# A fused attention and two-network kernel: a 32x32 inverse kept in PSUM, background work handed out by time, and filler matmuls two by two at two points

## The chip, the cores and the metric

One NeuronCore of one Trainium2 chip. The metric is the device time of one execution in microseconds (us); several executions are taken and their median is compared. The profile is one further execution, taken by the hardware profiler.

## What is computed

A linear-recurrence attention over 4 batches of 8 heads, 768 tokens, head width 40 (so 320 columns per token), and then two feed-forward networks on all 3,072 tokens:

```
for t in range(S):
    y[:, :, t] = einsum('bhd,bhde->bhe', rt, state)
    Sa = einsum('bhde,bhe->bhd', state, at)
    state = state * wt[:, :, None, :] - einsum('bhd,bhe->bhde', Sa, bt)
    state = state + einsum('bhd,bhe->bhde', vt, kt)
x = (sigmoid(y @ w_gate) * (y @ w_val)) @ w_out          # 320 -> 1536 -> 320
h = x @ w_in; e = exp(h - max(h)); u = h * e / sum(e)    # 320 -> 1024
out = layernorm(u) * g_ln @ w_out2                       # 1024 -> 320
```

## The kernel before, in words

**Slots.** The recurrence is done in 24 chunks of 32 tokens (`CH`), each for two halves of the heads, so in 48 half-chunks. `Attention.slot(s)` is written out for s from -6 to 48: slot s does the dependent part of half-chunk s and, ten slots ahead (`LOOK`), the preparation of a later one. A slot is a list `work` of ten points: 0 `m_r` and `m_st`; 1 and 2 the two halves of `m_ruv` of the half-chunk before, whose result VectorE masks into RL (L370); 3 `m_u` (ScalarE copies its PSUM result into Z at L312); 4 and 5 `products` of half-chunk s+9; 6 `m_y`, which reads RL; 7 `m_state`, which reads Z; 8 `m_ut`, `natural` and loads; 9 nothing. All engines work through their own instructions in the order in which the program issues them, and SyncE's queue issues the DMAs in that order.

**The inverse.** Each pair of chunks (n = 0 to 11, two chunks each) needs a 32x32 triangular inverse per head and chunk. `products` gives the matrices, ScalarE copies them to `abn` (L218), a DMA stores them to `ab`, and `t_load` loads them back as M (L526) in the layout that the inverse wants. `eye` loads a unit matrix from DRAM into the SBUF tile TT (two buffers). `t_iter(n, j)`, j = 0 to 30, does on VectorE one multiplication (L260: PSUM tile pT <- TT times M, both in SBUF) and one addition (L264: TT <- TT plus pT) on (j//2+1)*(31-j) columns. For n = 0 and 2 each is cut into two instructions from j = 6 on; for n = 1 VectorE takes the first two rows and GpSimd the rest (with an SBUF tile `tmp`). `t_store` writes TT to DRAM (L270), and `t_fetch` (L284) loads it as TB for `m_u`. `SOLVE` says which j are done in which of the four slots k = 0 to 3 that precede the use of inverse n; k = (s+5) mod 4.

**The background list.** `back` is a slot's list of VectorE work that no matmul of this slot waits for: the inverse's instructions and, in slots with k = 2 and 3, ahead of them, the four steps of `decay` (a clamp L144, two scans L154 and L161, two small ones). At each of the ten points the same number of items is handed out (`share`, the rest divided by the points left). In the k = 0 slot twelve empty items stand first, so that M has time to arrive. The list goes to `Between.fill`, which mixes it with the conversion of weights (`Convert.value`: four VectorE instructions L600 to L605 and two, L606 and L607, on the engine `cv.eng`, which is VectorE up to slot 2 and GpSimd after).

**The first network's units.** From slot 6 on, `fill` also puts in units of the first network for tokens that are finished: `units` yields in turn a gate (8 matmuls, L820), a value (8 matmuls, then a sigmoid on ScalarE L840 and a product on VectorE L841) and a third that splits the product (ScalarE L536, GpSimd L537) and does the 6 output matmuls (L853 to L855) of the tile before. One unit stands at each of the points `UNITS`; where none is ready, two dummy matmuls. After slot 48 the rest of the first network (`Late.tail`, `Late.first`) and the second (`Late.second`) follow.

Of the kernel before, what the change touches and what calls it, by code (L numbers as in the profile page):

```python
# [68 lines left out]
class Attention:  # L69
    def __init__(self, tc, ctx, d, xT, abd, ttd, bad, ident, zero, memory):  # L70
# [172 lines left out]

    def t_load(self, n):
        nc = self.nc
        M = self.sb.tile([128, CH, CH], F32, tag="M", name=f"M{n}", bufs=2)
        twice(nc, M.rearrange("p j t -> p (j t)"), self.abd[n])
        self.T[n] = (M, self.T.get(n) or self.eye(n))

    def t_iter(self, n, j):  # L250
# [5 lines left out]
        cut = min(m, T1) if n == 1 else m // 2 if m >= 4 and n in (0, 2) else 0
        parts = [(nc.vector, slice(0, cut), self.pT), (nc.gpsimd if n == 1 else nc.vector, slice(cut, m), self.tmp if n == 1 else self.pT)][cut == 0:1 + (cut < m)]

        def mult(eng, r, tmp):
            eng.tensor_tensor(out=tmp[:, 0:m * k].rearrange("p (c t) -> p c t", t=k)[:, r], in0=TT[:, r, j:j + 1].broadcast_to([128, r.stop - r.start, k]),  # L260
                              in1=M[:, j:j + 1, j + 1:CH].broadcast_to([128, r.stop - r.start, k]), op=ALU.mult)
# [1246 lines left out]
```

## Time and profile before

| | |
|---|---|
| Runs | 1168.12, 1170.61, 1173.04 us: median 1170.61 us |
| The profiled execution | 1175.68 us, of it 1173.9 us from first to last instruction |
| Busy share of the span | TensorE 88%, VectorE 72%, ScalarE 50%, GpSimd 41% |
| Slots 7 to 34 | from 197.3 to 538.9 us |
| Slots 39 to 47 | from 581.6 to some 664 us |
| Last part, without attention | from 684.0 us on |

Times in the profile count from the span's start. In the lines of groups the columns are: line, engine, operation, output <- inputs by the program's names, shapes, count | busy time in us, mean of one in ns | idle time of the engine before them and what ended it.

### The profile page before, as it was taken

The page shows a single profiled execution, that of the slowest core. Times are in us where ns is not written, and L with a number is a line of the kernel's source. Part 1 is how long each engine was busy: PE and PEld are TensorE (multiplying, and loading weights), DVE is VectorE, ACT ScalarE, POOL GpSimd, SP SyncE. Part 2 cuts the span into 40 slices and gives each one's busy share as a digit, 9 for nine tenths or more (in the row PEclk, how much of TensorE's full clock was granted, in tenths as well). Part 3 has the DMA queues.
Part 4 walks back from the last instruction along what each step waited for, and adds up shares of the span by engine and source line. Part 5 has one row for each costly group of instructions (what it writes and reads, how often), then busy time and mean ns, then how long its engine had stood idle before and what let it go on. Part 6 is the DMA issues. An engine that isn't in the chain of part 4 may idle for free.

```text
span 1173.9 us, 31891 instructions
## 1 busy us (share of the span) xinstructions
PE 1038.1 (88%) x12710; PEld 885.7 (75%) x12710; DVE 845.6 (72%) x2099; ACT 582.7 (50%) x1487; POOL 486.8 (41%) x529
## 2 busy tenths in 40 slices
PE   5527868898988989899999989799999998999997
PEld 2414546787877979788889878688888876888897
DVE  8969999999989898999894236234443359676673
ACT  4215534566656656656666435233443343544552
POOL 7628652644556455565321112144344301222232
PEclk8557987999999899989999989989999999999999
DMA  6455644667768665785564144312211000000001
GB/s 181 130 129 138 159 91 110 163 157 185 188 164 197 162 173 149 174 221 139 136 158 124 58 116 138 102 29 88 82 47 45 1 1 6 18 23 18 18 23 38
DMA packets 181037, 125.53 MB, mean 107 GB/s; under 512 B 106192, under 2 KB 159440, under 8 KB 180880
## 3 DMA queue, kind: packets, MB, share of 16 engines
q1 hardware_dynamic: 180880, 123.40, 40.1%
q8 instruction: 103, 1.69, 0.6%
q14 instruction: 54, 0.44, 0.1%
HBM read 101.83 MB, written 21.53 MB: 105 GB/s over the span
## 4 chain that ended last, share of the span: by engine, by line
PE 57%; DVE 24%; DMA 7%; ACT 4%; SPq 4%; issue 3%; POOL 1%; ACTq 0%; DVEq 0%; POOLq 0%
PE hid L820 20%; DVE pT L260 6%; PE one L820 5%; DVE TT L264 3%; PE pY L383 3%; PE two L853 2%; PE pruv L366 2%; PE three L1191 2%; PE three L1194 2%; PE three L1192 2%; PE two L855 2%; PE two L854 2%; PE two L1178 2%; PE pABK L206 2%; DVE G L161 2%
## 5 line engine op out<-in xcount | busy, mean ns | idle before, releaser
L260 DVE TENSOR_TENSOR pT<-TT,M 128x30 f32<-128x30 f32 (+38 forms) x422 | 161.2, 382 | 15.6 <-DMA TT<-in_ceye_dram 7.0
L820 PE MATMUL hid<-l_x,l_w 128*128 128x512 f32 x672 | 161.4, 392 | 0.0
L820 PEld LDWEIGHTS hid<-l_x,l_w 128*128 128x128 f32 x672 | 125.4, 189 | 24.4 <-issue 0.2
L820 PE MATMUL one<-b_tokens,b_w 128*128 128x256 f32 x816 | 125.2, 296 | 2.1 <-DVE b_plain L841 2.1
L223 POOL TENSOR_TENSOR AT<-abn,mA 64x256 f32<-64x256 f32 x96 | 79.4, 827 | 102.5 <-ACT abn L218 95.1
L820 PEld LDWEIGHTS one<-b_tokens,b_w 128*128 128x128 f32 x816 | 104.4, 191 | 7.7 <-DVE b_plain L841 2.3
L537 POOL TENSOR_TENSOR l_x<-l_plain,l_x 128x512 fp32r<-128x512 f32 x43 | 55.7, 1295 | 118.9 <-ACT l_x L536 99.9
L264 DVE TENSOR_TENSOR TT<-TT,pT 128x30 f32<-128x30 f32 (+38 forms) x422 | 94.6, 233 | 12.0
L841 DVE TENSOR_TENSOR l_plain<-hid,l_plain 128x512 f32<-128x512 f32 x43 | 29.7, 691 | 95.6 <-ACT l_plain L840 95.5
L383 PE MATMUL pY<-RL,YR 128*64 128x32 f32 (+1 forms) x1536 | 62.7, 226 | 39.8 <-DVE RL L370 38.3
L537 POOL TENSOR_TENSOR b_tokens<-b_plain,b_tokens 128x256 fp32r<-128x256 f32 x58 | 45.3, 780 | 123.2 <-ACT b_tokens L536 119.2
L820 PE MATMUL hid<-b_w,l_x 128*128 128x512 f32 x384 | 94.0, 397 | 2.6 <-DVE l_e L1150 2.6
L383 PEld LDWEIGHTS pY<-RL,YR 128*64 128x64 f32 (+1 forms) x1536 | 55.6, 137 | 51.7 <-issue 24.6
L820 PEld LDWEIGHTS hid<-b_w,l_x 128*128 128x128 f32 x384 | 70.9, 188 | 19.0 <-DVE l_e L1150 3.4
L206 PE MATMUL pABK<-AT,BK 128*64 128x64 f32 x768 | 62.8, 240 | 22.5 <-POOL BK L196 21.6
L195 POOL TENSOR_TENSOR AT<-AT,G 40x256 f32<-40x256 f32 x90 | 75.3, 837 | 15.6 <-DMA AT<-in_LA_dram 12.4
L206 PEld LDWEIGHTS pABK<-AT,BK 128*64 128x64 f32 x768 | 54.8, 151 | 33.9 <-POOL BK L196 24.2
L536 ACT ACTIVATE b_tokens<-b_plain 128x256 fp32r<-128x256 f32 (+1 forms) x70 | 33.7, 489 | 87.3 <-DVE b_plain L841 64.0
L312 ACT ACTIVATE Z<-pu 32x160 f32<-32x160 f32 x192 | 56.7, 295 | 34.4 <-PE pu L309 31.8
L840 ACT ACTIVATE l_plain<-hid 128x512 f32<-128x512 f32 x43 | 25.7, 597 | 96.5 <-PE hid L820 96.4
L935 PE MATMUL one<-zero 128*128 128x512 bf16 x196 | 66.7, 450 | 1.3 <-DVE lim L96 1.3
L1185 POOL TENSOR_TENSOR l_w<-l_e,l_w 128x1024 fp32r<-128x1024 f32 x12 | 28.8, 2403 | 89.1 <-ACT l_e L1146 51.1
(254 smaller groups left out, 2614.0 us busy)
## 6 DMA issues: line engine op xcount, KB each, us to landing
AT<-in_LA_dram SPq DMA_DIRECT2D x48, 256.0 KB
RL<-in_RS_dram SPq DMA_DIRECT2D x24, 512.0 KB
LB<-in_LB_dram SPq DMA_DIRECT2D x46, 208.0 KB
Z<-in_VN_dram SPq DMA_DIRECT2D x48, 160.0 KB
M<-ab SPq DMA_DIRECT2D x24, 256.0 KB
UV<-in_VT_dram SPq DMA_DIRECT2D x24, 208.0 KB
G<-in_LW_dram SPq DMA_DIRECT2D x22, 214.5 KB
xT<-yt SPq DMA_DIRECT2D x24, 160.0 KB
```

Of the source, the lines that this page charges most:

```text
L195: eng.tensor_tensor(out=at[SROW[g], g], in0=at[SROW[g], g], in1=G[SROW[g]], op=ALU.mult)
L206: yield lambda m=m: nc.tensor.matmul(ps[0:64, m * 64:m * 64 + 64], lhsT=bkt[:, m].rearrange("p s t -> p (s t)"), rhs=at[:, :, m, :], start ...
L223: nc.gpsimd.tensor_tensor(out=at[UROW[g], g].rearrange("p (a b) t -> p a b t", a=2), in0=abn[UROW[g], :, hs], in1=self.mA[UROW[g]].unsquee ...
L260: eng.tensor_tensor(out=tmp[:, 0:m * k].rearrange("p (c t) -> p c t", t=k)[:, r], in0=TT[:, r, j:j + 1].broadcast_to([128, r.stop - r.star ...
L264: eng.tensor_tensor(out=TT[:, r, j + 1:CH], in0=TT[:, r, j + 1:CH], in1=tmp[:, 0:m * k].rearrange("p (c t) -> p c t", t=k)[:, r], op=ALU.add)
L312: nc.scalar.activation(z[32 * q:32 * q + 32, hs, g, p * 4:p * 4 + 4, :], ps[32 * q:32 * q + 32, 0:160].rearrange("p (h d) -> p h d", d=40) ...
L383: yield lambda m=m, g=g, at=at: nc.tensor.matmul(ps[rows[g], m * CH:m * CH + CH], lhsT=flat[:, at:at + rows[g].stop - rows[g].start], rhs= ...
L536: nc.scalar.activation(h, src, AF.Copy)
L537: eng_l.tensor_tensor(out=l, in0=src, in1=h.bitcast(F32), op=ALU.subtract)
L820: nc.tensor.matmul(out, lhsT=a, rhs=b, start=n == 0, stop=n == 7)
L841: self.nc.vector.tensor_tensor(out=self.sg, in0=self.pv, in1=self.sg, op=ALU.mult)
L935: self.nc.tensor.matmul(self.gv, lhsT=z[:, 0:128], rhs=z, start=True, stop=True)
```

## The change

- `pT`, the PSUM tile of one bank, holds the inverse itself; the products go to one of two SBUF tiles `tmp`. So each multiplication reads PSUM and SBUF and writes SBUF, and each addition reads PSUM and SBUF and writes PSUM, in place.
- The unit matrix is loaded once into an SBUF tile and copied into pT by ScalarE (`eye`); `t_store` copies pT to SBUF by ScalarE, lets ScalarE write the next unit matrix, and stores as before. For n >= 1 it becomes an item of `back` in the k = 3 slot, behind the inverse's last step; for n = 1 that is slot 2 in place of slot 3.
- Inverse 1 is done by VectorE alone, in whole instructions; the conversions' last two instructions go to GpSimd in all slots.
- `back` carries an estimated time for each item, and each point gets its share of the remaining time (items are taken until the share is used up). The twelve empty items become one of 2.0 us. The steps of `decay` stand behind the inverse's, no longer ahead of them. `SOLVE` for n >= 3 gives 12, 12, 4 and 3 steps to k = 0 to 3 in place of 6, 9, 8 and 8. Counted through for n >= 3: in a k = 0 slot the empty item fills point 0 and the inverse begins at point 1; in k = 2 and 3 slots the inverse's instructions fill points 0 to 2 or 0 and 1, `t_store` stands at point 2 of k = 3, and `decay` at points 2 to 5.
- `m_state` at the end of a pair of chunks adds in place in PSUM, and the product with PE reads that PSUM tile.
- `UNITS` becomes (2, 2, 9, 9): two units at point 2 and two at point 9.

```diff
-SOLVE = (0, 0, 13, 26, 31), (0, 0, 11, 21, 31), (0, 6, 15, 23, 31)
-T1 = 2
-STORE = 5
+SOLVE = (0, 0, 13, 26, 31), (0, 0, 11, 21, 31), (0, 12, 24, 28, 31)
+WAIT = 2.0
-UNITS = (2, 5, 7, 9)
-LAST = {-2: (2, 7, 9), -1: (2, 7, 9), 0: (2,)}
+UNITS = (2, 2, 9, 9)
+LAST = {-2: (2, 9, 9), -1: (2, 9, 9), 0: (2,)}
...
-    def eye(self, n):
-        TT = self.T[n] = self.sb.tile([128, CH // 2, CH], F32, tag="TT", name=f"TT{n}", bufs=2)
-        self.nc.sync.dma_start(out=TT.rearrange("p j t -> p (j t)"), in_=self.d["ceye"])
-        return TT
+    def eye(self):
+        self.nc.scalar.activation(self.pT, self.unit, AF.Copy)
...
+        M, TT = self.M[n], self.pT.rearrange("p (j t) -> p j t", t=CH)
         k, m = CH - 1 - j, j // 2 + 1
+        tmp = self.tmp[j % 2][:, 0:m * k].rearrange("p (c t) -> p c t", t=k)
+        cut = m // 2 if m >= 4 and n in (0, 2) else 0
+        parts = [r for r in (slice(0, cut), slice(cut, m)) if r.stop > r.start]
+        def mult(r):
+            nc.vector.tensor_tensor(out=tmp[:, r], in0=TT[:, r, j:j + 1].broadcast_to([128, r.stop - r.start, k]),
+                                    in1=M[:, j:j + 1, j + 1:CH].broadcast_to([128, r.stop - r.start, k]), op=ALU.mult)
+        def add(r):
+            nc.vector.tensor_tensor(out=TT[:, r, j + 1:CH], in0=TT[:, r, j + 1:CH], in1=tmp[:, r], op=ALU.add)
+        return [(0.155 + (r.stop - r.start) * k * 0.00104, lambda r=r, f=f: f(r)) for f in (mult, add) for r in parts]
...
     def t_store(self, n):
+        self.M.pop(n)
+        TT = self.sb.tile([128, CH // 2, CH], F32, tag="TT", name=f"TT{n}", bufs=1)
+        self.nc.scalar.activation(TT.rearrange("p j t -> p (j t)"), self.pT, AF.Copy)
+        if n + 1 < NSS:
+            self.eye()
...
-            nc.vector.tensor_tensor(out=o, in0=ps[SROW[g], 0:320].rearrange("p (n d) -> p n d", d=40), in1=z[SROW[g], hs, g], op=ALU.add)
+            nc.vector.tensor_tensor(out=sums if end else o, in0=sums, in1=z[SROW[g], hs, g], op=ALU.add)
-                nc.vector.tensor_tensor(out=o, in0=o, in1=pe.unsqueeze(2).broadcast_to([40, 8, 40]), op=ALU.mult)
+                nc.vector.tensor_tensor(out=o, in0=sums, in1=pe.unsqueeze(2).broadcast_to([40, 8, 40]), op=ALU.mult)
...
-                back += [None] * (12 if s >= 0 else 0)
+                back += [(WAIT, None)]
...
+            if k == 2 * SS - 1:
+                back += [(0.0, lambda: self.t_store(n))]
...
-                back = self.decay(m, hs) + back
+                back += zip((0.5, 1.3, 0.4, 1.3), self.decay(m, hs))
...
-            share = -(-len(back) // (len(work) - p))
-            fill(s, back[:share])
-            back = back[share:]
+            share, left = [], sum(x for x, _ in back) / (len(work) - p)
+            while back and (left > 0 or p == len(work) - 1):
+                x, f = back.pop(0)
+                share.append(f)
+                left -= x
+            fill(s, share)
...
-            self.cv.eng = self.nc.vector if s < 3 else self.nc.gpsimd
+            self.cv.eng = self.nc.gpsimd
```

## Rows read from the trace of the kernel before

**Rows 1.** Busy time by stretch (from:to, length; PE, PEld, DVE, ACT, POOL; PEclk, DMA):

```profile
31.50:64.40 32.90, 15.94 (x128) 10.86 (x126) 29.94 (x114) 8.72 (x21) 15.85 (x20) 0.60 0.43 113
81.20:197.30 116.10, 89.00 (x1279) 56.93 (x1278) 108.69 (x290) 56.35 (x165) 69.50 (x103) 0.84 0.55 138
197.30:538.90 341.60, 310.85 (x5905) 275.59 (x5904) 315.57 (x824) 213.30 (x638) 191.96 (x222) 0.93 0.66 168
...
306.90:317.30 10.40, 10.40 (x217) 9.46 (x217) 9.88 (x30) 7.68 (x24) 5.36 (x7) 1.00 0.59 163
329.00:345.10 16.10, 12.10 (x214) 11.00 (x214) 15.45 (x41) 9.66 (x30) 8.62 (x10) 0.89 0.48 136
```

**Rows 2.** Who waited for whom (us in total, times, longest):

```profile
PE pY L383 <- DVE RL L370: 38.3, 18, 4.9
...
ACT b_tokens L536 <- DVE b_plain L841: 64.0, 32, 8.9
```

**Rows 3.** Timeline of TensorE: `m_y` of slot 18, and the start of slot 39:

```profile
338.81 1.63 PE L383 MATMUL pY<-RL,YR 128*64 128x32 f32 x32 [2.72 <-DVE RL L370]
...
581.61 0.49 PE L295 MATMUL pr<-Z,AT 128*32 128x40 f32 x32
```

**Rows 4.** The chain that ended last, in order of time (start, length):

```profile
65.07 2.91 DMA tt<-TT
...
137.34 3.34 DMA tt<-TT
...
583.12 4.26 DMA M<-ab
```

**Rows 5.** Timeline of GpSimd and VectorE, the same shape early and later:

```profile
32.98 1.18 POOL L196 TENSOR_TENSOR BK<-LB,Q 104x512 f32<-104x512 f32 x1
...
33.21 1.03 DVE L260 TENSOR_TENSOR pT<-TT,M 128x58 f32<-128x58 f32 x1
...
82.20 0.23 DVE L260 TENSOR_TENSOR pT<-TT,M 128x58 f32<-128x58 f32 x1
...
82.46 0.22 DVE L264 TENSOR_TENSOR TT<-TT,pT 128x58 f32<-128x58 f32 x1
```

**Rows 6.** The inverse's two groups on VectorE from 31.5 to 64.4 us:

```profile
L260 DVE TENSOR_TENSOR pT<-TT,M 128x60 f32<-128x60 f32 (+33 forms) x56 | 20.5, 365 | 1.9
...
L264 DVE TENSOR_TENSOR TT<-TT,pT 128x60 f32<-128x60 f32 (+33 forms) x56 | 9.4, 205 | 1.1
```

**Rows 7.** Groups of VectorE from 81.2 to 197.3 us:

```profile
L260 DVE TENSOR_TENSOR pT<-TT,M 128x60 f32<-128x60 f32 (+32 forms) x81 | 32.4, 400 | 8.7 <-DMA TT<-in_ceye_dram 7.0
L264 DVE TENSOR_TENSOR TT<-TT,pT 128x60 f32<-128x60 f32 (+31 forms) x79 | 14.1, 198 | 1.3
...
L607 DVE TENSOR_TENSOR b_raw<-b_plain 128x384 f32<-128x384 f32 (+1 forms) x5 | 2.8, 553 | 0.0
```

**Rows 8.** The inverse's additions over one whole inverse, 296.4 to 345.1 us:

```profile
L264 DVE TENSOR_TENSOR TT<-TT,pT 128x126 f32<-128x126 f32 (+22 forms) x32 | 8.0, 250 | 1.1
```

**Rows 9.** Groups of VectorE from 197.3 to 538.9 us:

```profile
L260 DVE TENSOR_TENSOR pT<-TT,M 128x126 f32<-128x126 f32 (+23 forms) x221 | 84.5, 382 | 2.8
L264 DVE TENSOR_TENSOR TT<-TT,pT 128x126 f32<-128x126 f32 (+24 forms) x222 | 54.9, 249 | 7.4
...
L332 DVE TENSOR_TENSOR Z<-Z,PE 40x320 f32<-40x320 f32 x29 | 19.6, 675 | 1.0
```

**Rows 10.** A group of ScalarE, PSUM to SBUF, 512 columns:

```profile
L840 ACT ACTIVATE l_plain<-hid 128x512 f32<-128x512 f32 x43 | 25.7, 597 | 96.5 <-PE hid L820 96.4
```

**Rows 11.** Timeline of slot 16: `m_u`, ScalarE's copies, `m_y`'s successor `m_state`:

```profile
310.00 0.49 PE L309 MATMUL pu<-rn,TB 32*32 32x40 f32 x32
...
310.56 1.25 ACT L312 ACTIVATE Z<-pu 32x160 f32<-32x160 f32 x4 [0.44 <-PE pu L309]
...
313.69 0.81 PE L326 MATMUL pS<-Z,YR 64*40 64x40 f32 x32
```

**Rows 12.** The page's group of gate and value matmuls (8 to a unit):

```profile
L820 PE MATMUL one<-b_tokens,b_w 128*128 128x256 f32 x816 | 125.2, 296 | 2.1 <-DVE b_plain L841 2.1
```

More of the change, by code (lines that the diff above doesn't have):

```diff
@@ L91, in __init__ @@
         self.pT = py.tile([128, 512], F32, name="pT")
-        self.tmp = cp.tile([128, 160], F32, name="tmp")
+        self.unit = cp.tile([128, 512], F32, name="unit")
+        self.tmp = [cp.tile([128, 160], F32, name=f"tmp{i}") for i in range(2)]
         self.QB = [cp.tile([104, 8, WCOLS], F32, name=f"Q{i}") for i in range(3)]
@@ L105, in __init__ @@
         nc.sync.dma_start(out=self.ident, in_=d["cid"])
+        nc.sync.dma_start(out=self.unit, in_=d["ceye"])
         nc.sync.dma_start(out=self.mA, in_=d["cmA"].rearrange("p (n t) -> p n t", t=CH))
@@ L250, in t_iter @@
     def t_iter(self, n, j):
         nc = self.nc
-        M, TT = self.T[n]
+        M, TT = self.M[n], self.pT.rearrange("p (j t) -> p j t", t=CH)
         k, m = CH - 1 - j, j // 2 + 1
[L256 to L261, printed above, removed]
@@ L263, in add @@
-        def add(eng, r, tmp):
-            eng.tensor_tensor(out=TT[:, r, j + 1:CH], in0=TT[:, r, j + 1:CH], in1=tmp[:, 0:m * k].rearrange("p (c t) -> p c t", t=k)[:, r], op=ALU.add)
-        return [lambda x=x, f=f: f(*x) for f in (mult, add) for x in parts]
-    def t_store(self, n):
-        M, TT = self.T.pop(n)
+        tmp = self.tmp[j % 2][:, 0:m * k].rearrange("p (c t) -> p c t", t=k)
+        cut = m // 2 if m >= 4 and n in (0, 2) else 0
+        parts = [r for r in (slice(0, cut), slice(cut, m)) if r.stop > r.start]
@@ L328, in m_state @@
             o = zn[SROW[g], hs, g]
[L329 to L330 removed]
+            end = c % SS == SS - 1
+            sums = ps[SROW[g], 0:320].rearrange("p (n d) -> p n d", d=40)
+            nc.vector.tensor_tensor(out=sums if end else o, in0=sums, in1=z[SROW[g], hs, g], op=ALU.add)
+            if end:
                 pe = self.PE[c // SS + 1, hs][SROW[g]]
[L332 removed]
+                nc.vector.tensor_tensor(out=o, in0=sums, in1=pe.unsqueeze(2).broadcast_to([40, 8, 40]), op=ALU.mult)
     def m_ut(self, i):
@@ L479, in slot @@
                 self.t_load(pj // (2 * SS))
-            if s == 3 and p == STORE:
-                self.t_store(1)
             if p == 4 and s % 2 and 3 < s < NHS - 1:
@@ L488, in slot @@
                     self.w_sums(m, hs)
-            share = -(-len(back) // (len(work) - p))
-            fill(s, back[:share])
-            back = back[share:]
-        if 1 < n < NSS and k == 3:
-            self.t_store(n)
+            share, left = [], sum(x for x, _ in back) / (len(work) - p)
[4 more added lines that the diff above has]
+            fill(s, share)
         if s == -3:
@@ L955, in fill @@
         b, k = divmod(s - FILL, 4)
-        if p in LAST.get(s - NHS, UNITS) and not self.step(b):
-            self.dummy(IDLE)
+        for _ in range(LAST.get(s - NHS, UNITS).count(p)):
+            if not self.step(b):
+                self.dummy(IDLE)
         mix(self.jobs2.next if not self.jobs2.over() or self.jobs2.todo else lambda: next(flat.run, None), LATER[self.jobs2.over()][p], other)
```

13 lines of the change are left out of this document (4 added, 9 removed).

## The prediction

> **What bounds the kernel now.** I read the stretches first, then the waits, then the chain and the timeline inside each stretch. Three stretches hang on VectorE. From 31.5 to 64.4 us it does inverse 0 almost alone, busy 29.9 of 32.9 us. From 81.2 to 197.3 us (slots 0 to 6) it is busy 108.7 of 116.1 us, and in slots 7 to 34 315.6 of 341.6 us [rows 1]. A slot that runs freely takes 10.4 us, all of it TensorE at full clock; slot 18 takes 16.1 us, with VectorE busy for 15.45 and the granted clock at 0.89 [rows 1]. The place where TensorE loses it is point 6: `m_y` waits for RL 18 times, 38.3 us in all [rows 2], 2.72 us of it in slot 18 [rows 3], because the two masks behind `m_ruv` stand in VectorE's queue behind `decay` and the inverse. So 28 slots at 10.4 us, 291 us, is TensorE's floor for the long stretch, and VectorE's load is what keeps the kernel 50 us above it. In the first stretch the chain runs through inverse 0 into its store at 65.07 us [rows 4], and SyncE's queue, with everything behind that store, stands until then. After 538.9 us TensorE rules, and the change leaves that part as it is but for nine slots.
>
> **Why a multiplication is dear.** A multiplication of 58 columns at 33.21 us took 1.03 us and ended when GpSimd's instruction beside it had ended (32.98 + 1.18 = 34.16); the same shape at 82.20 us took 0.23 us, and the addition of that shape, which reads PSUM and SBUF, 0.22 us [rows 5]. The additions' means in the groups below stay at that level in stretches where GpSimd is busy half the time and more. So the cost is two SBUF inputs beside GpSimd, and the change takes exactly that away: no instruction of the inverse has two SBUF inputs any more. I price each new multiplication as an addition of its shape.
>
> **First stretch.** Inverse 0: 56 multiplications of 365 ns become 56 of 205 ns [rows 6], 56 x 0.160 = **-9.0 us**, all on the chain. (The additions' busy time is 9.4 us and not 56 x 0.205 = 11.5, so pairs overlap; if multiplications came to overlap as well, it would be 11.1: one end of the range.) ScalarE's copy out of PSUM before the store costs 0.6 us by a copy of 512 columns [rows 10], **+0.6**. The copy of the unit matrix into PSUM has no row; the nearest is that same 0.6 us. It lies behind the store's copy, off the chain, where ScalarE waits for SyncE's queue anyway. The unit matrix for inverse 1 no longer comes by a DMA: VectorE waited 7.0 us for it [rows 7]. M is issued just ahead of it in the same queue, so most of that wait stays: **-1**, bounds 0 and -7.
>
> **Slots 0 to 6.** Inverses 1 and 2 cost VectorE 32.4 + 14.1 = 46.5 us [rows 7]. After: inverse 1 whole and on VectorE alone is two times a whole inverse's additions, 2 x 8.0 [rows 8]; inverse 2 in halves is, like inverse 0, 2 x 11.5. 39.0 in all, -7.5. L606 and L607 leave VectorE, twice 2.8 us [rows 7], -5.6. The four products with PE lose some 0.2 us each, as below. **-14 us** of 108.7; with VectorE 94% busy I take all of it off the span. GpSimd, busy 69.5 of 116 [rows 1], loses its share of inverse 1 and gets those conversions, so it is no new bound. The store of inverse 1 comes a slot earlier; its 3.34 us on the chain [rows 4] may go (0 to -3.3, I take 0, as VectorE fills the time).
>
> **Slots 7 to 34.** 221 multiplications cost 84.5 us, as many additions 54.9: -29.6. L332 takes 675 ns for 320 columns with two SBUF inputs [rows 9]; with one in PSUM I take 490, from the additions' slope, -5.3. VectorE's busy time becomes 280.7; with the same 26 us idle, 307 us, above TensorE's 291. So it can give 35 us, 50 if VectorE stopped mattering. The order helps: RL no longer has two scans in front of it but a few small instructions, so the waits of rows 2 should nearly go, and `decay`, now behind RL, has a whole slot before GpSimd's products need it. Three things take back. (1) M: the wait of 2.0 us fills one point only, so the inverse begins at point 1, where it began at about 4. For inverse 11 M landed at 583.12 + 4.26 = 587.38, 5.8 us after its slot began [rows 3, 4], and point 1 comes some 1.3 us after that start (`m_r` takes 0.49, as much again for the transposes). RL stands behind that wait. Bounds 0 and 4.5 us for each of 7 inverses; I take 0.7, near the low end, as VectorE runs behind TensorE wherever it is the bound: 5 us. (2) The store's copy stands at point 2 of a k = 3 slot on ScalarE, waits for the last addition, and has `m_u`'s copies to Z behind it; 0 to 1.6 us each, I take 0.2. (3) Pairing: where a value and the splitting unit now stand at one point, ScalarE's split waits for VectorE's product at once; it waits 64 us now [rows 2], hidden. Between the end of `m_u` and `m_state` there were 3.2 us and the copies needed 1.3 [rows 11]; a unit of 8 matmuls, 125.2/102 = 1.2 us [rows 12], leaves this gap, so 2.0 stay: 0.7 to spare, no cost, with point 9's and point 2's covers longer by one unit. Sum **-29 us**.
>
> **Slots 38 to 47.** From slot 39 `products` are gone and `m_u` to `m_state` has `m_y` alone, some 1.0 us (3.2 less the unit and the products), against 1.3: +0.3 in each of nine, **+2.5**; the earlier store of inverse 11 gives **-1**.
>
> **Sum.** -9.0 + 0.6 - 1 - 14 - 29 + 2.5 - 1 = -50.9. The profiled execution took 1175.7 us (span 1173.9), 5.1 above the median; it would take 1124.8, and the median of 1170.6 becomes **1120**.
>
> **Rivals.**
> (a) PSUM costs more. Against: the 0.22 and 0.23 us of rows 5 are the same with and without a PSUM input. If each of the 56 + 87 + 222 multiplications took 65 ns more, 24 us would go back: 1144, chance 0.06. [...]
> (b) Reading and writing one PSUM bank in the same addition runs at half pace; no row shows such an instruction. An inverse's additions stream for 8.0 - 31 x 0.155 = 3.2 us; ten inverses on the chain give back 32: 1152, chance 0.08.
> (c) M is the next bound: 4.5 us for 7 inverses in place of 0.7, 27 back: 1147. For: the landing of inverse 11. Against: between `m_ruv` and `m_y` TensorE has some 3.8 us of work (two units 2.4, `m_u` 0.5, products 0.9). Chance 0.18.
> (d) **Slower**: ScalarE's queue at point 3. The gap there shrinks to 2.0 us, and the copies to Z may start late behind the split of a unit put at point 2. Each of the 33 slots 6 to 38 stalls by what the lateness has over 0.7 us; at 2.2 us the whole gain is spent, at 3 us it is 33 x 2.3 = 76: 1196. Against: in slot 16 the copies began 0.07 us after `m_u` ended [rows 11]. Chance 0.06.
> (e) The list does not hand out what it says, since VectorE's lengths depend on GpSimd; then the waits of the long stretch stay, and of its 29 us only L332's 5 are left: 24 back, 1144, chance 0.05.
> (f) VectorE stops mattering in slots 7 to 34: 21 us more, 1099, chance 0.07.
>
> **How the numbers follow.** The forecast has 0.50. Its own range, 1106 to 1134, comes from the overlap of pairs (-2), the unit matrix (-6), the store of inverse 1 (-3.3), and M and ScalarE (up to +14). The range of 8 in 10 takes in (a), (c), (e) and (f) and stops short of (b) and (d): 1098 to 1150. A measurement can tell some 0.5%, 6 us. Faster 0.90; slower, (d), 0.06; within 0.5%, where (b) and (c) come together, 0.04.
>
> **What would show it.** L260's mean at about the additions' 205 to 250 ns in all three stretches, beside GpSimd too (else a; L264 grown means b); inverse 0's store some 8 us earlier; the wait of `m_y` for RL nearly gone and slots of k = 2 and 3 near 10.4 to 11.5 us at full clock; no large wait of L260 for M (else c), of L326 for Z (else d). The forecast is wrong if VectorE's busy time falls by 35 us in slots 7 to 34 and the stretch does not.

## The result: 0.9% slower, with the profile after

The median of the changed kernel is 1181.1 us (1178.0 to 1184.0, 6 runs) beside 1171.2 us for the kernel before on the same chip (1168.1 to 1173.0, 6 runs). The ratio is 1.0091, interval 1.0074 to 1.0109. The forecast was 1120, faster, and its range ended at 1150. The profiled execution has a span of 1178.4 us, 4.5 above the one before; that one took 5.1 us more than its median, so the stretches below show less than the 9.9 us between the medians.

A slot's length below runs from its first matmul into `pr` to the next slot's. So measured, the stretches of the two profiled executions differ like this (before, after, in us):

```
                                    before   after    change
to the start of slot 7              197.3    181.0    -16.3
slots 7 to 34                       341.6    356.1    +14.5
slot 35 to the end of attention     145.1    153.9     +8.8
behind the attention                489.9    487.4     -2.5
```

The first line went the way of the forecast, though by less (-23.4); the second is where the forecast fell. VectorE's groups of the changed kernel answer to [rows 6, 9]; first from 31.5 to 64.4 us, then from 197.3 to 538.9 us:

```profile
L262 DVE TENSOR_TENSOR pT<-pT,tmp 128x60 f32<-128x60 f32 (+33 forms) x56 | 12.3, 219 | 1.9
L258 DVE TENSOR_TENSOR tmp<-pT,M 128x60 f32<-128x60 f32 (+33 forms) x56 | 9.5, 206 | 1.0
...
L262 DVE TENSOR_TENSOR pT<-pT,tmp 128x126 f32<-128x126 f32 (+22 forms) x208 | 54.4, 261 | 6.0
L258 DVE TENSOR_TENSOR tmp<-pT,M 128x126 f32<-128x126 f32 (+22 forms) x207 | 52.1, 252 | 32.6 <-DMA M<-ab 27.7
...
L336 DVE TENSOR_TENSOR Z<-pS,PE 40x320 f32<-40x320 f32 x27 | 13.2, 489 | 0.9
```

The multiplication is L258 now, the addition L262. A multiplication fell from 382 to 252 ns in the long stretch and from 365 to 206 in the first: the price was right. But the last column of L258 is new: VectorE stood 27.7 us in this stretch ahead of multiplications, waiting for M. Over the whole span, from the table of waits (us in total, times, longest), the wait for M in the kernel before was:

```profile
DVE pT L260 <- DMA M<-ab: 1.3, 1, 1.3
```

In the changed kernel, the last two lines beside [rows 2]:

```profile
DVE tmp L258 <- DMA M<-ab: 45.6, 9, 6.5
...
PE pY L387 <- DVE RL L374: 24.4, 17, 3.4
...
ACT b_tokens L539 <- DVE b_plain L844: 68.6, 38, 5.5
```

One of the nine waits for M, 5.6 us, is inverse 1's in slot 0; the other eight stand in the k = 0 slots 11 to 39, 3.9 to 6.5 us each.

By stretch (columns as in [rows 1]): the long one by clock time and by slots (7 to 34), then slot 19, a k = 0 slot, and slot 20 behind it:

```profile
197.30:538.90 341.60, 297.17 (x5697) 265.45 (x5695) 275.90 (x783) 213.94 (x629) 178.09 (x211) 0.92 0.63 156
181.00:537.10 356.10, 309.06 (x5904) 276.36 (x5904) 290.04 (x825) 224.43 (x660) 186.43 (x220) 0.91 0.64 158
334.40:349.90 15.50, 12.00 (x219) 10.87 (x220) 9.33 (x33) 7.05 (x21) 8.88 (x12) 0.89 0.93 239
349.90:359.80 9.90, 9.90 (x213) 9.20 (x212) 9.27 (x33) 7.12 (x21) 3.87 (x6) 1.00 0.16 39
```

For the same 28 slots VectorE is busy 290.0 us where it was 315.6 [rows 1], and idle 66 where it was 26. The multiplications and L336 gave the 35 us of the forecast (84.5 and 19.6 us [rows 9] became 54.7 and 14.2), but the other groups took some 10 us more. Slot 20, which nothing delays, takes 9.9 us. Slot 19 takes 15.5 with hardly more work in it (219 matmuls for 213). Of the 5.6 us between them 2.1 are TensorE's own, 12.0 us busy in place of 9.9: its granted clock was 1.00 from 334.4 to 345.0 us, where it was busy for 7.1 of 10.6 us, and 0.50 from 345.0 to 348.4 us, right behind its waits.

What happens in slot 19 can be read off three timelines, VectorE's, ScalarE's and TensorE's:

```profile
340.81 0.19 DVE L258 TENSOR_TENSOR tmp<-pT,M 128x31 f32<-128x31 f32 x1 [5.49 <-DMA M<-ab]
...
341.71 0.87 DVE L374 TENSOR_TENSOR RL<-pruv,mR 64x256 f32<-64x256 f32 x2
342.51 0.41 DVE L844 TENSOR_TENSOR b_plain<-one,b_plain 128x256 f32<-128x256 f32 x1
```

```profile
337.74 0.39 ACT L843 ACTIVATE b_plain<-one 128x256 f32<-128x256 f32 x1 [1.56 <-PE one L823]
342.95 0.42 ACT L539 ACTIVATE b_tokens<-b_plain 128x256 fp32r<-128x256 f32 x1 [4.82 <-DVE b_plain L844]
...
343.86 1.21 ACT L314 ACTIVATE Z<-pu 32x160 f32<-32x160 f32 x4
```

```profile
338.45 0.49 PE L311 MATMUL pu<-rn,TB 32*32 32x40 f32 x32
...
342.28 1.36 PE L387 MATMUL pY<-RL,YR 128*64 128x32 f32 x32 [2.27 <-DVE RL L374]
344.80 1.16 PE L328 MATMUL pS<-Z,YR 64*40 64x40 f32 x32 [1.15 <-ACT Z L314]
```

The first multiplication of inverse 6 reaches the head of VectorE's queue at 335.3 us; M lands at 340.7. Behind it in that queue stand RL and the product L844 of the unit at point 2. Behind the product, on ScalarE, stands the split L539, which the pairing has put at the same point, and behind the split the copies to Z. So TensorE meets one wait by two roads, as RL in `m_y` and as Z in `m_state`: Z is ready 6.1 us after `m_u`'s end where 1.3 is the free time, [rows 11] of before. The chain of waits through slots 18 and 19 (pieces of it, start and length in us) has become a chain of transfers, the tokens' into slot 18 and M's into slot 19:

```profile
313.50 6.14 DMA b_plain<-xT
...
333.38 1.66 DMA ab<-abn
...
335.70 4.98 DMA M<-ab
...
341.71 0.42 DVE RL L374
...
342.58 0.34 DVE b_plain L844
```

M's transfer is among the chain's longest pieces eight times, in the k = 0 slots 11 to 39, 4.0 to 5.0 us each; before it was there once [rows 4].

### The profile page after: what moved, and what is told of

It is laid out like the page before. It is cut to its first block, busy times and chain, and to the rows that moved or that the text cites. A ratio compares the mean times of both kernels' runs of the same rounds, so it can differ in the third digit from the quotient of the medians.

```text
span 1178.4 us, 31810 instructions
## 1 busy us (share of the span) xinstructions
PE 1033.0 (88%) x12710; PEld 884.5 (75%) x12710; DVE 793.4 (67%) x2085; ACT 595.7 (51%) x1511; POOL 468.6 (40%) x489
## 4 chain that ended last, share of the span: by engine, by line
PE 49%; DVE 25%; DMA 11%; ACT 6%; SPq 4%; issue 4%; POOL 1%; DVEq 0%; ACTq 0%; POOLq 0%
PE hid L823 20%; DVE pT L262 6%; DVE tmp L258 6%; PE one L823 5%; DMA M<-ab 3%; PE pruv L370 2%; DMA b_plain<-xT 2%; PE three L1195 2%; PE three L1198 2%; PE three L1196 2%; DMA ab<-abn 2%; DVE RL L374 2%; PE two L1182 2%; PE two L858 2%; PE two L856 1%
## 5 line engine op out<-in xcount | busy, mean ns | idle before, releaser
L258 DVE TENSOR_TENSOR tmp<-pT,M 128x30 f32<-128x30 f32 (+34 forms) x422 | 96.8, 239 | 54.5 <-DMA M<-ab 45.6
L224 POOL TENSOR_TENSOR AT<-abn,mA 64x256 f32<-64x256 f32 x96 | 90.1, 939 | 78.4 <-ACT abn L219 73.7
L823 PEld LDWEIGHTS one<-b_tokens,b_w 128*128 128x128 f32 x816 | 113.7, 210 | 6.5 <-DVE b_plain L844 4.3
L262 DVE TENSOR_TENSOR pT<-pT,tmp 128x30 f32<-128x30 f32 (+34 forms) x422 | 105.2, 249 | 12.4
L844 DVE TENSOR_TENSOR l_plain<-hid,l_plain 128x512 f32<-128x512 f32 x43 | 29.7, 691 | 94.9 <-ACT l_plain L843 94.9
L539 ACT ACTIVATE b_tokens<-b_plain 128x256 fp32r<-128x256 f32 (+1 forms) x70 | 34.1, 487 | 100.1 <-DVE b_plain L844 68.6
L387 PE MATMUL pY<-RL,YR 128*64 128x32 f32 (+1 forms) x1536 | 61.2, 221 | 26.5 <-DVE RL L374 24.4
L387 PEld LDWEIGHTS pY<-RL,YR 128*64 128x64 f32 (+1 forms) x1536 | 53.8, 132 | 33.6 <-issue 19.6
L196 POOL TENSOR_TENSOR AT<-AT,G 40x256 f32<-40x256 f32 x90 | 66.1, 734 | 21.8 <-DVE G L162 15.4
L370 PE MATMUL pruv<-RL,UV 128*64 128x64 f32 x768 | 62.5, 240 | 5.4 <-ACT YR L237 1.9
L370 PEld LDWEIGHTS pruv<-RL,UV 128*64 128x64 f32 x768 | 54.7, 151 | 14.5 <-issue 3.0
```

The source lines that it names most:

```text
L196: eng.tensor_tensor(out=at[SROW[g], g], in0=at[SROW[g], g], in1=G[SROW[g]], op=ALU.mult)
L224: nc.gpsimd.tensor_tensor(out=at[UROW[g], g].rearrange("p (a b) t -> p a b t", a=2), in0=abn[UROW[g], :, hs], in1=self.mA[UROW[g]].unsquee ...
L258: nc.vector.tensor_tensor(out=tmp[:, r], in0=TT[:, r, j:j + 1].broadcast_to([128, r.stop - r.start, k]), in1=M[:, j:j + 1, j + 1:CH].broad ...
L262: nc.vector.tensor_tensor(out=TT[:, r, j + 1:CH], in0=TT[:, r, j + 1:CH], in1=tmp[:, r], op=ALU.add)
L370: yield lambda p=p, hh=hh, m=m: nc.tensor.matmul(ps[0:64, m * 64:m * 64 + 64], lhsT=uvt[:, hs * 4 + hh, 64 * p:64 * p + 64], rhs=rl[:, hs, ...
L387: yield lambda m=m, g=g, at=at: nc.tensor.matmul(ps[rows[g], m * CH:m * CH + CH], lhsT=flat[:, at:at + rows[g].stop - rows[g].start], rhs= ...
```

## The experiments

Eighteen kernels ran, each timed in three rounds. The table gives, per kernel, its median, the ratio to the kernel before with its interval, the mean length of the slots 8 to 38 by their place k in the four slots of an inverse, and the time from the start of slot 7 to that of slot 35 (both of the profiled execution). A difference of 0.01 in the ratio is 11.7 us.

```
                      median  ratio  interval       k=0   k=1   k=2   k=3   slots 7-34
before                1171           -              10.6  10.7  12.7  13.7  341.6
after                 1181.1  1.0091 1.0074-1.0109  15.1  10.5  11.3  13.6  356.1
e1_wait5              1168.2  0.9966 0.9943-0.9989  10.5  13.6  10.9  13.1  345.3
e2_units              1162.2  0.9912 0.9879-0.9944  12.0  12.2  10.8  12.5  336.3
e3_wait5_units        1157.3  0.9890 0.9852-0.9928  10.9  11.6  11.0  13.1  334.4
e4_oldlist_units      1141.2  0.9732 0.9697-0.9768  11.3  10.5   9.8  14.0  324.9
e5_decay6             1140.9  0.9724 0.9689-0.9758  12.3  10.5   9.7  13.7  329.0
e6_oldlist_paired     1146.2  0.9786 0.9747-0.9825  11.0  10.2  10.6  14.0  328.3
e7_decay6_ready9      1145.9  0.9776 0.9742-0.9811  11.0  10.6   9.7  14.7  325.6
e9_store_later        1137.7  0.9715 0.9661-0.9770  11.2  11.4   9.7  13.7  326.1
e10_store_sums_later  1143.2  0.9772 0.9737-0.9807  11.6  11.6   9.7  13.4  328.0
e11_all_paired        1159.6  0.9898 0.9861-0.9935  12.8  10.5  10.4  14.9  348.7
e12_wait5_steps       1159.7  0.9895 0.9840-0.9951  10.2  10.4   9.8  17.6  346.9
e13_level             1142.8  0.9766 0.9742-0.9790  11.9  10.7  10.3  13.2  325.5
e14_level_paired      1153.6  0.9863 0.9840-0.9886  12.2  10.1  11.0  14.0  334.8
e15_early             1142.3  0.9763 0.9742-0.9784  11.3  10.7   9.7  13.9  323.9
e16_bytime            1142.9  0.9755 0.9726-0.9783  11.5  10.7   9.6  14.0  329.8
e17_no_ready          1132.5  0.9678 0.9647-0.9709  11.4  10.7  10.0  12.2  313.6
e18_no_decay1         1129.2  0.9630 0.9597-0.9663  10.7  11.0   9.8  13.4  319.6
```

**e1_wait5**, the inverse begins later:

```diff
-                back += [(WAIT, None)]
+                back += [(1.0, None)] * (5 if s >= 0 else 2)
```

> The changed kernel with five empty entries of 1.0 us in place of the one WAIT of 2.0 ahead of inverses 2 to 11, so that an inverse begins at point 4 of its k = 0 slot. Theory 1 (the wait for M at the head of VectorE's queue, 45.6 us in 9 waits, holds RL and the product of the units and so makes the k = 0 slots 14.3 to 16.6 us long): the waits for M fall below 8 us, the k = 0 slots 11 to 39 fall to 10.4 to 11.5, some 8 x 4 = 32 us come off, 1181 becomes 1146 to 1155. Theory 2 (the pairing of the units is the loss, the wait for M is only where VectorE waits meanwhile): within 6 us of 1181, the k = 0 slots stay above 13.5. Theory 3 (both wait in turn): 1160 to 1172.

Measured: 0.9966 for 1.0091, some 15 us. The waits for M fell to 15.6 us, 5.6 of them inverse 1's in slot 0 (theory 1 had below 8). The k = 0 slots fell to 10.5, as theory 1 says, but the k = 1 slots grew by 3.1 us, and the time landed in theory 3's range. Slot 20 (k = 1) shows where it went: TensorE's next gate waits for the product of a unit, and in VectorE's queue this product stands behind steps 6 to 10 of the inverse, which are left of slot 19's twelve. First slots 19 and 20 by stretch (columns as above), then TensorE's timeline, then VectorE's (126 columns are step 10):

```profile
327.10:338.10 11.00, 10.09 (x219) 9.35 (x219) 7.98 (x25) 7.04 (x21) 6.96 (x10) 1.00 0.80 210
338.10:351.90 13.80, 11.60 (x217) 10.53 (x216) 12.87 (x43) 7.40 (x22) 5.96 (x8) 0.88 0.53 129
```

```profile
343.47 2.08 PE L823 MATMUL one<-b_tokens,b_w 128*128 128x256 f32 x8 [2.20 <-DVE b_plain L844]
```

```profile
342.47 0.29 DVE L258 TENSOR_TENSOR tmp<-pT,M 128x126 f32<-128x126 f32 x1
...
343.00 0.41 DVE L844 TENSOR_TENSOR b_plain<-one,b_plain 128x256 f32<-128x256 f32 x1
```

**e2_units**, the units at four points again:

```diff
-UNITS = (2, 2, 9, 9)
-LAST = {-2: (2, 9, 9), -1: (2, 9, 9), 0: (2,)}
+UNITS = (2, 5, 7, 9)
+LAST = {-2: (2, 7, 9), -1: (2, 7, 9), 0: (2,)}
```

> The changed kernel with the first network's units at four points again (UNITS 2, 5, 7, 9 and LAST as before). Theory 1 (M): 1181 within 6 us, the waits for M stay at 40 us or more. Theory 2 (pairing: ScalarE's split of a unit waits for VectorE's product ahead of the copies to Z, 4.8 to 6.3 us after m_u in the k = 0 slots): Z comes within 2 us of m_u, the k = 0 slots fall to 11.5 or less, 1145 to 1155. Theory 3 (both): 1165 to 1175.

Measured: 0.9912, some 21 us, more than theory 3 gave it, less than theory 2. The wait for M is still there, but it no longer reaches Z: in slot 19 (a k = 0 slot again) the copies to Z follow `m_u` at once and the split comes behind them. First the wait, then ScalarE's timeline:

```profile
DVE tmp L258 <- DMA M<-ab: 26.8, 8, 5.0
```

```profile
328.79 1.20 ACT L314 ACTIVATE Z<-pu 32x160 f32<-32x160 f32 x4
...
332.44 0.42 ACT L539 ACTIVATE b_tokens<-b_plain 128x256 fp32r<-128x256 f32 x1 [1.32 <-DVE b_plain L844]
```

The k = 0 slots fell from 15.1 to 12.0, so of the 4.6 us by which they stood above 10.5, 3.1 went with the pairing and 1.5 stayed. How much of the 3.1 is the road through the product and Z is not shown: the waits for M in these slots became shorter too (1.8 to 4.6 us), and the k = 1 slots grew from 10.5 to 12.2.

**e3_wait5_units**, both edits:

> Both edits: the inverse begins at point 4 and the units stand at four points. Theory 1: as the run with the later beginning alone, within 6 us of it (1146 to 1155). Theory 2: as the run with the four points alone. Theory 3: faster than either by over 10 us, 1135 to 1145. What stays in the k = 3 slots (11 to 17.8 us now) is in all three theories ScalarE's wait for the tokens that the next block's splitting loads, and is not touched here.

Measured: 0.9890, no more than e2 alone within the intervals, and not the 1135 to 1145 of theory 3. With the units at four points the wait for M is worth little by itself.

**e4_oldlist_units**, the inverse in PSUM without the new order:

```diff
-SOLVE = (0, 0, 13, 26, 31), (0, 0, 11, 21, 31), (0, 12, 24, 28, 31)
+SOLVE = (0, 0, 13, 26, 31), (0, 0, 11, 21, 31), (0, 6, 15, 23, 31)
-                back += [(WAIT, None)]
+                back += [(1.0, None)] * (12 if s >= 0 else 0)
-                back += zip((0.5, 1.3, 0.4, 1.3), self.decay(m, hs))
+                back = [(1.0, f) for f in self.decay(m, hs)] + back
...
+            many = -(-len(back) // (len(work) - p))
+            fill(s, [f for _, f in back[:many]])
+            back = back[many:]
```

with UNITS and LAST as in e2.

> The inverse in PSUM alone (with its conversions on GpSimd and L336 in PSUM): the list is handed out by count as before, decay first, twelve empty entries ahead of an inverse, the old steps per slot, the units at four points. If the price of the multiplications was worth what was forecast, this alone gives 1171 - 50 = 1121 to 1135. If VectorE was no longer what held the k = 2 and k = 3 slots once its work was cheaper (ScalarE's wait for the tokens' load in them), it gives only the first stretch, inverse 0 and slots 0 to 6: 1145 to 1155.

Measured: 0.9732, 31 us faster than before, and 42 us faster than the change that contains it. It lies between the two theories: the first stretch and slots 0 to 6 gave 14.0 us (slot 7 began at 183.3), the long stretch 16.7. Over the long stretch both engines are now idle for part of the time, TensorE for 25 us and VectorE for 42, but in slot 18 (k = 3) VectorE is busy for 14.45 of 15.1 us. The rows are slots 7 to 34, then slot 18:

```profile
183.30:508.20 324.90, 300.17 (x5905) 267.15 (x5904) 282.92 (x824) 219.05 (x650) 189.20 (x223) 0.96 0.67 173
...
307.80:322.90 15.10, 12.35 (x215) 11.08 (x214) 14.45 (x39) 9.98 (x31) 7.54 (x9) 0.89 0.44 124
```

Three of the four slots are at TensorE's floor or near it (9.8 to 11.3 us); the k = 3 slots, at 14.0, have not moved.

**e5_decay6**, e4 with decay behind RL's point:

```diff
-                back = [(1.0, f) for f in self.decay(m, hs)] + back
+                back[6:6] = [(1.0, f) for f in self.decay(m, hs)]
```

> The kernel with the inverse in PSUM alone (its list handed out by count), with one thing moved: decay enters the list as its seventh entry, behind the point at which RL's masks are issued, and not ahead of everything. Theory 1 (in the k = 3 slots, 12.7 to 16.2 us there, RL waits behind decay's two long scans, and TensorE for RL): the waits of m_y for RL fall from 17.3 to below 6 us, the k = 3 slots to 11.5, some 8 x 3 = 24 us come off 1141: 1115 to 1125. Theory 2 (the k = 3 slots are long because ScalarE, late from the splitting of the next block's tokens, starts them late; RL is only what is seen last): within 6 us of 1141.

Measured: 0.9724, theory 2. The wait of `m_y` for RL fell from 17.3 to 5.3 us and nothing was won by it: the k = 3 slots fell by 0.3 us and the k = 0 slots grew by 1.0.

**e6_oldlist_paired**, e4 with the pairing of the change (against e4):

```diff
-UNITS = (2, 5, 7, 9)
-LAST = {-2: (2, 7, 9), -1: (2, 7, 9), 0: (2,)}
+UNITS = (2, 2, 9, 9)
+LAST = {-2: (2, 9, 9), -1: (2, 9, 9), 0: (2,)}
```

> The same kernel with the inverse in PSUM alone, its list by count and decay first, but the units two by two at two points as in the change. Theory 1 (pairing costs wherever the second unit's split waits for a product that stands in VectorE's queue behind part of the inverse): 10 to 25 us slower than 1141, 1151 to 1166, with the product's wait in more and longer pieces. Theory 2 (pairing costs only together with the wait for M, or with a list that starts an inverse with twelve steps): within 6 us of 1141, or up to 12 faster, since a slot that nothing delays takes 9.96 us in the changed kernel and 10.38 here.

Measured: 0.9786, 6 us slower than e4 with intervals that touch. Theory 2: beside the old list the pairing costs little. (Its slot lengths in the table are those of its fastest execution, 1138.1 us.)

**e7_decay6_ready9**, e5 with the token split at point 9:

```diff
-FIRST, NEXT = (1, 6), (0, 7)
+FIRST, NEXT = (1, 6), (0, 9)
```

> As the run with decay as seventh entry, with the splitting of the next block's tokens at point 9 of its slot in place of point 7, behind the copies to UV and YR. Theory 1 (RL alone makes the k = 3 slots long): within 6 us of that run. Theory 2 (ScalarE, waiting 15 to 29 us for these tokens' transfer with the copies for the next slot behind it, makes them long): the k = 3 slots fall by 2 to 3 us each, 15 to 25 us faster than that run.

Measured: 0.9776, theory 1's number, but inconclusive: ScalarE's wait for the tokens' transfer fell from 18.0 to 5.2 us, but now TensorE waited 10.9 us, 10 times, for the split tokens themselves.

**e8_before_paired**, the two lines of the change's UNITS and LAST in the kernel of before, is a miss of mine. In the kernel of before a point is tested for membership in UNITS, so (2, 2, 9, 9) issues one unit at each of two points there and leaves out half the units of every slot. It ran in 1220.5 us (ratio 1.0417, 1.0378 to 1.0457) and says nothing on pairing.

> The kernel of before with the pairing alone (UNITS 2, 2, 9, 9). Theory 1 (pairing itself costs wherever VectorE is behind): with VectorE 92% busy in slots 7 to 34, 10 to 30 us slower than 1171: 1181 to 1200. Theory 2 (it costs only with the wait for M at the head of VectorE's queue): 1165 to 1177.

**e9_store_later** (against e5, the first two edits) and **e10_store_sums_later** (all of them) clear ScalarE's queue ahead of `rn`:

```diff
-            if k == 2 * SS - 1:
-                back += [(0.0, lambda: self.t_store(n))]
+            if p == 3 and k == 0 and 1 < n <= NSS:
+                self.t_store(n - 1)
...
+                at = (len(back) + 4) * 4 // 10 + 4 if hs else 6
+                back += [(1.0, None)] * (at - len(back))
-                back[6:6] = [(1.0, f) for f in self.decay(m, hs)]
+                back[at:at] = [(1.0, f) for f in self.decay(m, hs)]
...
-            if p == SUMS[pi % 2]:
-                m, hs = divmod(pi + 2, 2 * SS)
-                if hs < 2 and (2, 0) < (m, hs) < (NSS, 0):
+            if pi % 2 == 0 and p in (4, 6):
+                m, hs = divmod(pi + 1 + p // 6, 2 * SS)
+                if hs == (p == 4) and (2, 0) < (m, hs) < (NSS, 0):
```

> The run with decay as seventh entry (1141), with the two ScalarE copies that follow an inverse (PSUM to TT, unit matrix to PSUM) moved from the end of the k = 3 slot to point 3 of the next, behind the copies to Z. Theory 1 (in the k = 0 slots rn stands on ScalarE behind the copy to TT, which waits for the inverse's last addition, 3.3 to 4.8 us after pr): rn comes within 1.5 us of pr there, the k = 0 slots fall from 11.5 to 14.2 to 10.4 to 11, 8 x 2 = 16 us off: 1122 to 1130. Theory 2 (VectorE, late at that place, is what TensorE then meets in another wait): within 6 us of 1141.

> As the run with the copies at point 3, and besides ScalarE's two sums of the next decay (L138, 2.5 us), which stand ahead of rn at the start of a k = 3 slot, moved to point 4 of that slot, behind the copies to Z, with decay behind them. Theory 1 (ScalarE's order makes the k = 3 slots long: rn comes 3.7 to 6.3 us after pr): the k = 3 slots fall by 2 us each, 10 to 18 us faster than the run with the copies alone. Theory 2 (VectorE's decay and inverse there are what counts): within 6 us of that run, or slower, since decay comes later.

Measured: 0.9715 and 0.9772, both theory 2. In e9 the k = 0 slots fell from e5's 12.3 to 11.2, and the k = 1 slots grew from 10.5 to 11.4. It has the lowest median of all versions that compute the whole, but its interval covers e4's.

**e11_all_paired**, e10 with the edit of e6:

> As the run with copies and sums moved, but with the units two by two as in the change. Theory 1 (pairing costs only what VectorE's late product makes of it; where nothing is late a slot takes 9.96 and not 10.38 us): 3 to 12 us faster than that run. Theory 2 (pairing costs by itself): 5 to 15 us slower.

Measured: 0.9898, 15 us slower than e10, theory 2. So e6 did not settle it: the same pairing costs 6 us beside one order and 15 beside another.

**e12_wait5_steps**, e1 with the old steps per slot:

```diff
-SOLVE = (0, 0, 13, 26, 31), (0, 0, 11, 21, 31), (0, 12, 24, 28, 31)
+SOLVE = (0, 0, 13, 26, 31), (0, 0, 11, 21, 31), (0, 6, 15, 23, 31)
```

> The changed kernel (units paired, list by time, decay behind the inverse, its copies at its end) with five empty entries ahead of an inverse and the steps per slot as before the change (6, 9, 8 and 8 in place of 12, 12, 4 and 3). The run with the five entries alone took 1168, the one with list and steps of old and the pairing 1146. Theory 1 (the steps: twelve in a k = 1 slot, 12.9 to 16.2 us long there, hold the second unit's product): k = 1 slots near 10.4, 1142 to 1152. Theory 2 (the handing-out by time and the place of decay): within 6 us of 1168.

Measured: 0.9895, between the theories. The k = 1 slots came down to 10.4 as theory 1 says, and the k = 3 slots went up to 17.6, where decay stands behind eight steps. In slot 22 there, 20.1 us long, TensorE waits 1.95 us for Z and 1.71 us for `yt` (L392), and on VectorE each stands directly behind a scan of decay. That this is the whole of the rise is not shown.

**e13_level** and **e14_level_paired**, e5 and its form with the edit of e6:

```diff
-SOLVE = (0, 0, 13, 26, 31), (0, 0, 11, 21, 31), (0, 6, 15, 23, 31)
+SOLVE = (0, 0, 13, 26, 31), (0, 0, 11, 21, 31), (0, 8, 18, 27, 31)
```

> The run with the list by count and decay as seventh entry (1141), with the steps of an inverse per slot 8, 10, 9 and 4 in place of 6, 9, 8 and 8. Theory 1 (VectorE still sets the period of four slots, by its k = 3 slot alone: there it is busy 12.5 to 13.9 us, with decay, four sums and the token split, and 8.9 to 9.9 us in the other three): the k = 3 slots fall by 2 us to 11.5 or 12, the others grow by 0.5 at most, 1120 to 1132. Theory 2 (the k = 3 slots wait for ScalarE or the tokens' transfer): within 6 us of 1141.

> As the levelled run, with the units two by two. Theory 1 (the pairing costs where VectorE is late with the product, since the next unit writes the bank that this product reads): with VectorE level it costs nothing or gains up to 10 us against the levelled run. Theory 2 (it costs by itself, 16 to 19 us in two of the pairs of runs before): 10 to 20 us slower than the levelled run.

Measured: 0.9766 and 0.9863. Levelling took 0.5 us off the k = 3 slots and put 0.6 on the k = 2 slots: theory 2, no gain. The pairing costs 11 us here: theory 2 again.

**e15_early**, against e4:

```diff
-                back += [(1.0, None)] * (12 if s >= 0 else 0)
+                back += [(1.0, None)] * (3 if s >= 0 else 0)
```

> The kernel with the inverse in PSUM alone (1141: list by count, decay first, four points, old steps) with three empty entries ahead of an inverse in place of twelve, so that it begins at point 1 as in the change; nothing else differs. Theory 1 (beginning before M has landed costs by itself, through RL and the product behind the waiting multiplication): waits for M of 3 to 5 us in each of 9 inverses, the k = 0 slots 14 to 15.5 us in place of 11.3, 1165 to 1175. Theory 2 (the wait takes time that the k = 0 slot or the later ones give back, because VectorE's work that follows is done earlier): 1141 to 1152.

Measured: 0.9763, within the interval of e4. But the run hardly made the wait it was meant to make: VectorE waited for M 12.0 us in 3 waits, 7.0 of them in slot 0, and in slots 7 to 34 once, 2.1 us in slot 23. Slot 19 there, on VectorE:

```profile
325.06 0.19 DVE L258 TENSOR_TENSOR tmp<-pT,M 128x31 f32<-128x31 f32 x1 [1.30 <-ACT pT L241]
325.28 0.87 DVE L374 TENSOR_TENSOR RL<-pruv,mR 64x256 f32<-64x256 f32 x2
```

The multiplication waits for the unit matrix, not for M: the inverse before ends late, its copy and the new unit matrix come later still, and by then M is there. So cheap multiplications and an early beginning do not bring the wait out by themselves. e2 begins at the same point with its units at the same four points, and waits for M in seven k = 0 slots; it has the change's 12, 12, 4 and 3 steps, which leave little of the inverse to the k = 3 slot, and decay behind them.

**e16_bytime**, the changed kernel with the edits of e1, e2 and e12, and decay first in the list; against e4 the handing-out by time:

```diff
-                back += zip((0.5, 1.3, 0.4, 1.3), self.decay(m, hs))
+                back = list(zip((0.5, 1.3, 0.4, 1.3), self.decay(m, hs))) + back
```

> The kernel with the inverse in PSUM alone (1141: old steps, decay first, four points) with its list handed out by time, as the change does, and five entries of 1.0 us ahead of an inverse; the handing-out is all that differs. Theory 1 (the sharing by time costs by itself: the run with steps of old by time and paired was 1160, by count and paired 1146): 1150 to 1158. Theory 2 (what cost there was decay behind the inverse in the k = 3 slots, 17.6 us on average in that run): within 6 us of 1141.

Measured: 0.9755, theory 2. The handing-out by time costs nothing that these runs can tell.

**e17_no_ready** (the first edit, in `ready`) and **e18_no_decay1** (the others, in `decay` and at the call of `w_sums`) leave work out of e4's k = 3 slots:

```diff
-        split(self.nc, *self.X[b % 2], self.st, self.nc.vector)
+        if b < 2:
+            split(self.nc, *self.X[b % 2], self.st, self.nc.vector)
...
+        if hs and n > 2:
+            self.PE[n, hs], self.Q[n, hs], self.G[n, hs] = self.PE[n, 0], self.Q[n, 0], self.G[n, 0]
+            return []
...
-                if hs < 2 and (2, 0) < (m, hs) < (NSS, 0):
+                if hs < 2 - (m > 2) and (2, 0) < (m, hs) < (NSS, 0):
```

> The kernel with the inverse in PSUM alone (1141), with the splitting of the tokens left out for the blocks from the third on, so that the first network's units there read the tokens of an earlier block; its transfer stays. Theory 1 (ScalarE's wait for the tokens' transfer, 17 us in 6 waits, and the copies for the k = 3 slot behind it are what holds those slots at 14.0): the k = 3 slots fall to 12 or less, 1120 to 1128. Theory 2 (it is VectorE's decay and inverse there): VectorE saves 1.4 us in each, 1130 to 1140.

> The same kernel with the second decay of a pair of chunks (its two sums on ScalarE, 1.8 us, and its clamp and scans on VectorE, about 4 us, in a k = 3 slot) left out from the third pair on; the first one's results are read in its place. Theory 1 (ScalarE's wait for the tokens holds the k = 3 slots): 1128 to 1138. Theory 2 (VectorE's load in the k = 3 slots, of which this is the largest piece, sets the period of four slots): the k = 3 slots fall from 14.0 to 11 or less, 9 x 3 = 27 us off, 1110 to 1120.

Measured: 0.9678 and 0.9630, 6 and 12 us below e4 by the ratios (9 and 12 by the medians). In slots 7 to 34 it is the other way round: 11.3 us less than e4 without the token split and 5.3 without the decay, whose run began slot 7 some 7 us earlier already. Without the token split the k = 3 slots fell to 12.2, without the decay to 13.4, never to 11. Each run fell into the range of the theory that makes the piece left out the smaller one: so neither holds alone, and both pieces count. The two were not left out together.

## Why the prediction was wrong, by its own steps

**The prices were right.** "I price each new multiplication as an addition of its shape": 252 ns where the additions of before took 249 [rows 9], 206 in inverse 0 where they took 205 [rows 6]. L336 took 489 where 490 was taken. Rival (a) fell with that: no run shows the 65 ns more that it put on each multiplication. The means lie 3 and 1 ns above the additions', and a multiplication of 58 columns takes 0.20 to 0.22 us with one input in PSUM, where it took 0.23 with both in SBUF and GpSimd idle beside it (for 3.14 us, up to 83.08) [rows 5]. Rival (b) fell too, and no run shows its half pace: an addition that reads and writes one bank took 261 ns for 249, 2.5 us over 208 of them, and from 31 to 126 columns its mean grew from 198 to 294 ns, where before it grew from 187 to 286. Inverse 0 ended at 56.55 us and the transfer of its store began at 57.84, 7.2 us ahead of 65.07 [rows 4]; the forecast said some 8 us.

**First stretch and slots 0 to 6**: -16.3 us to slot 7 where the terms gave -23.4. Inverse 0 gave its share (slot 1 began 10.0 us earlier); slots 1 to 6 took 97.7 us for 104.0, 6 where 15 was forecast. VectorE's busy time there fell by 11, from 99.4 to 88.1, but its idle time grew from 4.6 to 9.6: "I take all of it off the span" was half right. TensorE's waits for VectorE in slots 1 to 6 did fall by 15 us, from 22.8 to 7.6, but its waits for ScalarE grew from 1.0 to 9.0. The longest, 4.2 us, is for the copy `abn` (L219), which stood behind a conversion that had waited 3.3 us for its weights.

**Slots 7 to 34** is the step that failed, at "(1) M ... I take 0.7, near the low end, as VectorE runs behind TensorE wherever it is the bound". The change took away that very lateness. With cheap multiplications and three steps in the k = 3 slot VectorE came to the k = 0 slot on time, and then waited 3.9 to 6.5 us in eight inverses. The upper bound given was 4.5, but M came 5.9 to 7.1 us into these slots and not 5.8. The prediction carried a premise from the trace of before over a change that made it false. And "(3) Pairing ... no cost" failed at the same place: the split waits for the product at once, as it said, and the product stands behind the multiplication that waits for M. In slots that nothing delays the gap was as forecast: Z 1.28 us and `m_state` 1.91 us after `m_u` in slot 20, against 1.3 and 2.0. Rivals (c) and (d) were priced as two cases, 27 us and 2.3 us in 33 slots. They were one chain: 4.6 us in each of eight k = 0 slots, some 37 us by slot lengths. Less than that can be won back: with the wait cut from 40 to 10 us in these slots (e1) they came down in full, but the k = 1 slots grew, and 15 us were won.

**"The order helps"** failed as well. `m_y`'s waits for RL went from 38.3 to 24.4 us where they "should nearly go", the k = 3 slots stayed at 13.6 us where 10.4 to 11.5 was forecast (in slot 18 the chain comes through the tokens' transfer, as shown above), and the new steps per slot with decay behind them cost 16 us (e16 against e3). In the old list, decay behind RL's point won nothing (e5).

**"The same 26 us idle"** failed even without the new order. In e4 VectorE's busy time for the 28 slots fell by 32.7 us, to 282.9, and the stretch by 16.7: idle time rose to 42. What was left sits in the k = 3 slots (14.0 us in e4): the token split and decay there both count (e17, e18), and levelling VectorE's steps won nothing (e13).

**Slots 38 to 47** were forecast at +1.5; slot 39 alone took 15.3 us for 9.7, inverse 11's wait for M. Behind it the pairing saves: slots 43 to 45 took 26.9 us for 27.5, not +0.3 each, and 26.9 in e6 for 27.8 in e4, which differ by the pairing alone.

**Where the gain went**, by the ratios and a time of 1170.6: the inverse in PSUM alone, with L336 and the conversions as in the change, is worth -31 us (e4). The new order gave +42 back. Of these, undoing the pairing returns 21, beginning later 15, both 24 (e2, e1, e3). The other 18 lie in the steps per slot together with decay's place behind them, since the handing-out by time is free (e16 against e3 leaves 16 for those two). Rival (e) fell with that. Not settled: why the pairing costs 6 us in one order and 11 to 15 in others, and what share of the k = 3 slots' 14 us is whose. That VectorE stopped mattering, rival (f), holds in e4 for three slots in four.

## What to carry to other kernels

When an engine gets cheaper and its work is moved, look at what it was late for: a wait that its lateness hid (here M's landing, some 6 us into the slot) can come out in full, so price it at its bound and not at what the old trace shows. Then follow what is queued behind the waiting instruction to the end, across engines: a wait at the head of one queue is dear by what others have since been placed behind it, and two rivals that meet in one instruction are one case. Where a change has a cheaper operation and a new order, the operation can be run alone in the old order: here that was worth 31 us and the whole cost 11.

## What the runs showed of the hardware

Pairs of half instructions. The prediction had the additions of such a pair overlapping. VectorE at the end of inverse 0, the timeline joining the two of a pair:

```profile
55.89 0.24 DVE L258 TENSOR_TENSOR tmp<-pT,M 128x8 f32<-128x8 f32 x2
56.17 0.38 DVE L262 TENSOR_TENSOR pT<-pT,tmp 128x8 f32<-128x8 f32 x2
```

Two multiplications from PSUM to SBUF took 0.24 us together, two additions in place in PSUM 0.38; one of this shape takes 0.16 and 0.17 us on the mean. So it is the pair of multiplications that overlaps now and the pair of additions that does not: over inverse 0 they cost 9.5 and 12.3 us, where before it was 20.5 and 9.4 [rows 6].

Waits and a lower clock behind them. Behind the two waits of slot 19 (2.27 and 1.15 us) TensorE's granted clock stood at 0.50 for 3.4 us; over the slot it was 0.89, and 219 matmuls took 12.0 us where 213 took 9.9 at 1.00 in the next slot. That the waits brought the lower clock is not shown.
